# Pack attention with a soft mixture of experts on one core: the third duo's sums, the token shares and the PSUM banks are put in other places

## The chip, the cores and the metric

The kernel runs on one core of a Trainium2 chip. The metric is the device time of one execution in microseconds (us). The five engines of the core have these names in the profile: PE (TensorE, matmuls), DVE (VectorE), ACT (ScalarE), POOL (GpSimd) and SP (SyncE), which issues all the transfers here. In the trace each engine runs its instructions in the order in which the program lists them, so an instruction that waits holds up what is listed behind it on that engine.

## The reference

```python
def attn(q, k, v, p):                 # q, k, v: 8 x 8 x 576 x 64, p: 8 x 8 x 32 x 64
    s = p @ k^T / 8;   a = softmax(s);   pp = a @ v         # pack: 32 rows per head
    s = q @ pp^T / 8;  a = softmax(s);   return a @ pp      # unpack: 576 rows per head
x = attn(...) as 4608 tokens x 512
logits = x @ phi                      # 4608 x 32 slots
d = softmax of logits over the tokens (axis 0)
slot_in = d^T @ x                     # 32 x 512; 4 slots belong to each of 8 experts
slot_out[e] = max(slot_in[e] @ w1[e], 0) @ w2[e]            # w1: 512x1024, w2: 1024x512
c = softmax of logits over the slots (axis 1)
out = c @ slot_out                    # 4608 x 512, float32
```

The tokens x are never formed: the logits are taken as a @ (pp @ phi), and the slot inputs are summed as d^T @ a, times pp.

## The kernel before

**Steps and duos.** The batch of 8 is worked through in four duos of two batches (`dd` = 0 to 3), and each duo in two steps of four heads (8 steps, `i` = 0 to 7, `ND` = 4). A step loads k, v and q, makes pack scores (L229), their softmax, the packed rows (L297), transposes q (L386), makes unpack scores (L430), their softmax (L457 to L480: maximum, difference, exponential on ACT, row sum and reciprocal on DVE, product on POOL), transposes the shares (L491, L502) and makes logits (L518, added up into `LT` by L535).

**Duo sums.** After the second step of a duo the softmax over the tokens goes on as a running one. F1, F2, F2d: maximum `mt` of the duo's logits, a transpose `mx` of it on PE, and a new running maximum `m4` with the difference `dm`. F3, F3d, F3x: two tiny matmuls `my` spread them over the partitions, DVE negates them (`nmg`), and ACT takes the exponentials `dL` with row sums `zg`. F4d: DVE transposes `dL` into `dz` and forms `rw`. F4: matmul `mz` adds up the row sums. F5: the logits are transposed into `L_sb`. GR: 36 matmuls `gr` (L654) multiply `dz` with the duo's shares. RTa, RTd: `gr` is copied to `rt` by ACT and by DVE. GT, GB, GS, GSA: two more small matmuls with a product `rb` between them, whose result is added to `S_run`. GZ keeps `z_run`, the running divisor; in the last duo it also scales `hm` and `S_run` by its reciprocal. After the last duo L921 puts `S_run` plus the last `gs` into `xz`, the experts' inputs; this is the last step before the experts.

**The order** of all these steps is written out by hand in the text `ORDER`, one word per step, and everything that a step issues goes on its engines in that order. The first step of duo 0's sums stands behind step 3's logits, of duo 1's behind step 5's. The loads of the weights are issued as slots of a ring of 14 tiles, or memory of tiles no longer needed (`GIVE`), come free.

**Token shares.** `c1`, `c2`, `c3` make the softmax of `L_sb` over the slots (two reductions of 1152 elements per partition, L937 and L949, a difference, an exponential, a product), `cq` splits it in two parts, and `cp` transposes it, four transposes (L1062) into one PSUM bank and a copy into `cT`; there are nine such groups.

**Experts.** `layer1a` (matmuls `hp`, L982) and `layer2` (`so`, L1031) go through 8 experts; `hidden` and `layer1b` copy and transpose between them. Expert 7's second layer is made in two halves (`sb`, L1108), then `sr` (L1121, L1129) adds up partitions, and `sh` is the slot output. The code from `layer1a` to `sh` keeps the order in which it is written.

**Output.** 36 tiles of 128 tokens: a matmul `op` of 128x512 (L1145; the first tile in two halves, L1162), a copy from PSUM by ACT or DVE (L87, L90, in the helper `evac`, which gives each copy to the engine with the smaller sum of estimated costs), and transfers of 1 MB from `ob`, the last two of 0.5 MB from `ot`. This part is not ordered by hand: a scheduler places its instructions, and did so with the last seven groups of `cp`.

**PSUM** has eight banks of 128x512. Before the experts: one pair of banks `m` (pool `psm`) and three rotating pairs (pool `prs`). In the experts and the output: two rotating pairs in pool `psa` (for `hp`, `sb`, `sr`, `op`), one bank for `so`, three single banks in pool `pstr` (for `ht`, `cp`). A pair is handed on only as a whole.

Of the kernel before, what the change touches and what calls it, by code (L numbers as in the profile page):

```python
# [20 lines left out]
def pack_attention_soft_moe(  # L21
# [586 lines left out]
    def f4(dd):  # L608
        x = du[dd]
        x["zp"] = pair(prs, f"mz_{dd}")[:, 0, 0:NSLOT]  # L610
        nc.tensor.matmul(x["zp"], ones, x["rw"], start=True, stop=True)
# [127 lines left out]
    def load_w(pool, lay, e, c):  # L739
# [92 lines left out]
        XQA.2 PREP.2 N2.1 MP.2 MXb.3 MM.2 S1a.3 EXb.3 MXa.3 QC.2 A2P.1 XQC.2 EXa.3 KT1.4 A2T.1
        S2.2 KT0.4 QE.3 AP.3 MT.2 MS.2 AT.3 A1T.3 LG.1 A1U.3 QC.3 PPM.3 XQC.3 E2.2 LT.1 F1.0
        F2.0 PPN.3 QA.3 F2d.0 QB.3 XQA.3 Z.2 F3.0 S1a.4 XQB.3 S1b.4 F3d.0 MXa.4 N2.2 F3x.0 F4d.0
        EXa.4 PT.3 MXb.4 PPT.3 F4.0 GR.0 QE.4 KT0.5 EXb.4 PRP.3 MP.3 RTa.0 AP.4 MM.3 PREP.3
        RTd.0 GZ.0 A1T.4 GT.0 KT1.5 S2.3 GB.0 GS.0 MT.3 AT.4 GSA.0 A2P.2 F5.0 A1U.4 MS.3 PPM.4
        A2T.2 QC.4 LG.2 E2.3 PPN.4 QB.4 LT.2 QE.5 Z.3 PT.4 XQC.4 XQB.4 QA.4 XQA.4 S1a.5 N2.3
        PPT.4 S1b.5 MXa.5 MP.4 EXa.5 MXb.5 MM.4 A2P.3 EXb.5 KT1.6 S2.4 A2T.3 KT0.6 AP.5 MT.4
        MS.4 AT.5 A1T.5 LG.3 A1U.5 QC.5 PPM.5 QE.6 XQC.5 E2.4 LT.3 F1.1 F2.1 PPN.5 QA.5 F2d.1
        QB.5 XQA.5 Z.4 F3.1 S1a.6 XQB.5 S1b.6 F3d.1 MXa.6 N2.4 F3x.1 F4d.1 EXa.6 PT.5 MXb.6  # L840
        PPT.5 F4.1 GR.1 KT0.7 EXb.6 MP.5 RTa.1 AP.6 MM.5 RTd.1 GZ.1 GT.1 A1T.6 S2.5 KT1.7 GB.1
        GS.1 MT.5 AT.6 GSA.1 A2P.4 F5.1 A1U.6 MS.5 PPM.6 A2T.4 QC.6 LG.4 E2.5 PPN.6 QE.7 QA.6
        LT.4 Z.5 PT.6 XQC.6 QB.6 PPT.6 XQA.6 MP.6 S1a.7 MM.6 XQB.6 N2.5 S1b.7 MXa.7 S2.6 EXa.7
        MXb.7 EXb.7 QA.7 MT.6 MS.6 AT.7 AP.7 A1U.7 XQA.7 QC.7 A1T.7 E2.6 A2P.5 PPM.7 XQC.7 Z.6
        A2T.5 QB.7 N2.6 PPN.7 LG.5 XQB.7 LT.5 PT.7 PPT.7 F1.2 F2.2 MP.7 F2d.2 MM.7 A2P.6 S2.7
        A2T.6 MS0.7 F3.2 LG.6 LT.6 MT.7 E20.7 MS1.7 E21.7 F3d.2 Z0.7 F3x.2 N20.7 Z1.7 A2P0.7
        N21.7 A2T0.7 A2P1.7 F4d.2 F5.2 A2T1.7 F4.2 GZ.2 LG.7 LT.7 GR.2 F1.3 F2.3 RTd.2 RTa.2
        GT.2 F2d.3 F3.3 GB.2 GS.2 F3d.3 F3x.3 GSA.2 F4d.3 F4.3 F5.3 GZ.3 GR.3 RTa.3 RTd.3 GT.3
        GB.3 GS.3 GSA.3
# [55 lines left out]
    with tc.manual_schedule(engines={EP.PE, EP.DVE, EP.Activation, EP.Pool}):  # L905
# [15 lines left out]
        nc.vector.tensor_tensor(  # L921
# [53 lines left out]
    def layer1a(e0, es):  # L975
        if e0 == es[0]:
            hp = pair(psa, f"hp_{e0}")
            hss[e0] = [hp[:, 0], hp[:, 1]]
        hp = hss[e0]
        for e in es:  # L980
            for nh, a in ((nh, 2 * c + y) for c in range(2) for nh in range(2) for y in range(2)):
                nc.tensor.matmul(  # L982
                    hp[nh][32 * a : 32 * a + 32, :],
                    xzf[:, (4 * e + a) * NSLOT : (4 * e + a + 1) * NSLOT],
                    w1s[e, a // 2][:, a % 2, nh * 512 : (nh + 1) * 512],
                    start=(e == e0),
                    stop=(e == e0 + QE - 1),
                )
# [222 lines left out]
```

## Time and profile before

| | |
|---|---|
| Time, median of 3 runs | 240.16 us (239.95 to 242.99) |
| The profiled execution | 241.48 us, span from first to last instruction 239.7 us |
| Busy | PE 192.1 us (80%), DVE 137.5 (57%), ACT 89.7 (37%), POOL 31.2 (13%) |
| Moved | 72.84 MB, of which 9.44 MB is output; mean 304 GB/s |
| Mean granted PE clock | 0.876 |

How to read it: the profiled execution's time is its span plus 1.8 us around it, and every duration below is from that one execution. The granted clock is the share of its full speed that PE was given; eight transposes of 128x128 took 1.09 us at a clock of 1.00 (at 134.8 us), four took 1.11 us at 0.50 (at 143.9 us). Start times are counted from the start of the span.

### The profile page before, as it was taken

What the parts mean: (1) busy time and instruction counts of PE and PEld (TensorE: products, weight loads), DVE (VectorE), ACT (ScalarE), POOL (GpSimd) and SP (SyncE); (2) the same over time, 40 slices, a digit from 0 to 9 for tenths busy, and PEclk for the clock granted to TensorE, in tenths of its full rate; (3) what the DMA queues carried; (4) which work ended last, traced back from release to release, by engine and by line L of the source; (5) the groups of instructions that cost most, each with busy time, mean ns of one, the idle gap of its engine ahead of it and who ended that gap; (6) DMA issues with size and microseconds to landing.
All of it is one profiled execution on the core that took longest, in us unless ns stands there. A gap on an engine that the chain in (4) does not pass through costs nothing.

```text
span 239.7 us, 6484 instructions
## 1 busy us (share of the span) xinstructions
PE 192.1 (80%) x2795; PEld 128.6 (54%) x2795; DVE 137.5 (57%) x280; ACT 89.7 (37%) x174; POOL 31.2 (13%) x42
## 2 busy tenths in 40 slices
PE   0569977899879999979998627874999999688960
PEld 0247666777649777769786515772233344233320
DVE  2563786678596689767776486396312634433240
ACT  2041736374472473643667332102020010444520
POOL 6103000521060030020223010100030000000000
PEclk9999999999997999979999995757899999855555
DMA  5999999999999999995592990086499992278767
GB/s 155 385 338 349 390 391 270 390 389 326 345 389 391 391 406 407 407 374 187 198 355 72 424 383 5 0 299 228 130 421 428 418 415 118 72 282 347 298 278 304
DMA packets 27037, 72.84 MB, mean 304 GB/s; under 512 B 6400, under 2 KB 6656, under 8 KB 24192
## 3 DMA queue, kind: packets, MB, share of 16 engines
q1 hardware_dynamic: 27008, 72.42, 81.7%
q8 instruction: 22, 0.36, 0.6%
q14 instruction: 7, 0.06, 0.1%
HBM read 62.98 MB, written 9.44 MB: 302 GB/s over the span
## 4 chain that ended last, share of the span: by engine, by line
PE 52%; DMA 18%; DVE 14%; ACT 8%; issue 3%; SPq 1%; POOL 0%; DVEq 0%; ACTq 0%
DMA pn<-in_p_dram 8%; PE gr L654 7%; PE hp L982 7%; DMA k<-in_k_dram 6%; PE op L1145 6%; PE so L1031 5%; PE m L297 5%; PE s L430 4%; PE s L229 4%; DMA q<-in_q_dram 4%; PE a2p L491 3%; PE ap L263 2%; DVE ob L90 2%; ACT ob L87 2%; DVE kT L212 2%
## 5 line engine op out<-in xcount | busy, mean ns | idle before, releaser
L229 PE MATMUL s<-kT,pT 32*32 32x288 f32 x512 | 20.7, 458 | 9.2 <-DVE kT L212 8.7
L1145 PE MATMUL op<-sh,cT 128*128 128x512 f32 x35 | 23.1, 744 | 2.9 <-DVE ob L90 1.3
L480 POOL TENSOR_TENSOR a<-a,z 128x1152 f32<-128x1152 f32 (+1 forms) x8 | 15.9, 1992 | 61.7 <-DVE nmg L588 19.0
L212 DVE STREAM_TRANSPOSE kT<-k 128x1152 f32<-128x1152 f32 x16 | 21.4, 1358 | 0.2
L297 PE MATMUL m<-v,a1T 64*64 64x128 f32 x576 | 19.8, 291 | 0.7 <-ACT a1T L287 0.4
L250 ACT ACTIVATE a<-s,nm 128x576 f32<-128x576 f32 x16 | 11.9, 742 | 19.5 <-DVE nm L240 13.4
L297 PEld LDWEIGHTS m<-v,a1T 64*64 64x64 f32 x576 | 17.5, 144 | 3.1 <-issue 1.2
L240 DVE TENSOR_REDUCE nm<-s 128x1 f32<-128x576 f32 x16 | 12.0, 755 | 11.1 <-PE s L229 11.1
L1145 PEld LDWEIGHTS op<-sh,cT 128*128 128x128 f32 x35 | 9.8, 279 | 15.8 <-ACT ob L87 7.3
L386 PE MATMUL qp<-ident,q 128*128 128x128 f32 x128 | 16.7, 276 | 1.2 <-issue 1.2
L229 PEld LDWEIGHTS s<-kT,pT 32*32 32x32 f32 x512 | 9.0, 111 | 15.6 <-DVE kT L212 9.6
L90 DVE COPY ob<-op 128x512 f32<-128x512 f32 (+1 forms) x13 | 8.6, 670 | 14.0 <-PE op L1145 13.5
L87 ACT COPY ob<-op 128x512 f32<-128x512 f32 (+1 forms) x20 | 11.4, 575 | 13.5 <-PE op L1145 11.7
L654 PE MATMUL gr<-a,dz 128*64 128x128 f32 x144 | 16.4, 398 | 0.0
L982 PE MATMUL hp<-w,xz 128*32 128x512 f32 x128 | 16.0, 649 | 0.5 <-DVE xz L921 0.5
L430 PE MATMUL s<-ppT,qT 128*64 128x64 f32 x512 | 16.3, 222 | 0.1
L391 ACT COPY qT<-qp 128x1024 f32<-128x1024 f32 x16 | 15.9, 1021 | 0.7 <-PE qp L386 0.6
L386 PEld LDWEIGHTS qp<-ident,q 128*128 128x128 f32 x128 | 14.0, 141 | 3.3 <-issue 2.7
L654 PEld LDWEIGHTS gr<-a,dz 128*64 128x64 f32 x144 | 15.2, 206 | 1.1 <-issue 0.9
L430 PEld LDWEIGHTS s<-ppT,qT 128*64 128x64 f32 x512 | 15.6, 138 | 0.2 <-ACT a L250 0.2
L491 PE MATMUL a2p<-ident,a 128*128 128x128 f32 x64 | 9.7, 296 | 5.5 <-POOL a L480 4.5
L457 DVE TENSOR_REDUCE mx<-s 128x32 f32<-128x1024 f32 (+1 forms) x9 | 9.9, 1096 | 6.0 <-PE s L430 6.0
(144 smaller groups left out, 283.0 us busy)
## 6 DMA issues: line engine op xcount, KB each, us to landing
w<-in_moe_w_dram SPq DMA_DIRECT2D x31, 1024.0 KB, 10.7
k<-in_k_dram SPq DMA_DIRECT2D x16, 576.0 KB, 8.4
v<-in_v_dram SPq DMA_DIRECT2D x16, 576.0 KB, 10.3
q<-in_q_dram SPq DMA_DIRECT2D x16, 576.0 KB, 11.6
out_dram<-ob SPq DMA_DIRECT2D x7, 1024.0 KB, 3.9
pn<-in_p_dram SPq DMA_DIRECT2D x16, 64.0 KB, 8.0
w<-in_moe_w_dram SPq DMA_DIRECT2D x2, 512.0 KB, 16.9
out_dram<-ot SPq DMA_DIRECT2D x2, 512.0 KB, 5.3
```

What stands on the lines that cost most here:

```text
L87: nc.scalar.copy(dst, src)
L212: nc.vector.transpose(st[i]["kT"][:, b2].rearrange("p a t x r -> p (a t x r)"), kts[i][:, b2].rearrange("p a x -> p (a x)"),)
L229: nc.tensor.matmul(ps[32 * c : 32 * c + 32, u, 0:HALF], pTs[dd][rs, b2, g, a, x], kT[rs, b2, a, :, x, :], start=(x == 0), stop=(x == 1),)
L297: nc.tensor.matmul(s["m"][64 * b2 : 64 * b2 + 64, y, 0:P], s["a1T"][rs, t, 64 * b2 : 64 * b2 + 64], vt[rs, b2, :, t * D : (t + 1) * D], st ...
L386: nc.tensor.transpose(tp[:, o : o + P], qts[i][:, b2, a, j * P : (j + 1) * P], ident)
L391: nc.scalar.copy(flat(qT(i)[:, 8 * b2 : 8 * b2 + 8]), st[i][f"qp{b2}"])
L430: nc.tensor.matmul(pv[64 * b2 : 64 * b2 + 64, j, h], s["qT"][:, 8 * b2 + 4 * a + j, R * y : R * y + R], ppT[:, b2, h], start=True, stop=True,)
L480: eng.tensor_tensor(a2, a2, st[i][f"z{t0}"].unsqueeze(3).broadcast_to([P, n, 4, NS]), op=ALU.mult)
L491: nc.tensor.transpose(s["ap2"][:, t * P : (t + 1) * P] if t < 8 else s["lp"][:, 1, 0:P], s["a2"][:, t].rearrange("p h s -> p (h s)"), ident,)
L654: nc.tensor.matmul(x["gb"][64 * c : 64 * c + 64, g * P : (g + 1) * P], dz[:, t].rearrange("p b s -> p (b s)"), a2[:, t].rearrange("p h s - ...
L982: nc.tensor.matmul(hp[nh][32 * a : 32 * a + 32, :], xzf[:, (4 * e + a) * NSLOT : (4 * e + a + 1) * NSLOT], w1s[e, a // 2][:, a % 2, nh * 5 ...
L1145: nc.tensor.matmul(op, cT[:, o, :], sh, start=True, stop=True)
```

## The change

**Order of the duo sums.** In duos 0 and 1, F3 to F4d stand earlier, right behind F2d and between the two halves of q's transposes, and GR stands ahead of F4. In duo 2, F3 to F4d stand ahead of the last step's softmax, and GR, F4, GT, GB and GS are placed among the steps of that softmax, where they stood behind it. In duo 3 likewise F4d is followed by F5 and GR, and only then come F4 and GZ. `mz` of duo 2 now takes the pair `m` (`psm`). On PE, from the first duo (`qp` are transposes of q, `s_4` pack scores, `ap` transposes of shares):

```order
-L386 MATMUL qp_1_983<-ident,q_185 128x128 x8
-L575 MATMUL my_999<-ones,m_0_979 128x1
-L229 MATMUL s_4_0_1001<-kT_840,pT_788 32x288 x16
-L229 MATMUL s_4_1_1019<-kT_840,pT_788 32x288 x16
+L575 MATMUL my_983<-ones,m_0_979 128x1
+L386 MATMUL qp_1_988<-ident,q_185 128x128 x8
+L229 MATMUL s_4_0_1010<-kT_840,pT_788 32x288 x16
+L229 MATMUL s_4_1_1028<-kT_840,pT_788 32x288 x16
 L341 MATMUL m_903<-ident,ppd_966 128x128 x2
-L611 MATMUL mz_1057<-rw_1046,ones 128x32
-L654 MATMUL gr_1059<-a_0_434,dz 64x128 x9
-L654 MATMUL gr_1059<-a_1_620,dz 64x128 x9
```

`my` has moved ahead of the second eight transposes of q, and behind these rows `gr` comes first and `mz` after it. Around the last softmax PE had, before (`s_7` are the last unpack scores, `a2p_2132` the transposes of the last shares, `lp_2133` the last logits, `gr_2163` duo 2's sums, `mx_2188` the transposed maximum of duo 3):

```order
-L430 MATMUL s_7_2050<-ppT,qT_1915 64x2x32 x32
-L575 MATMUL my_2099<-ones,m_2_2030 128x1
-L583 MATMUL my_2099<-dm_2032,ones 128x32
-L518 MATMUL lp_2039<-a2T_2093,mm_1814 32x288 x4
-L491 MATMUL a2p_2132<-ident,a_7_2049 128x128 x8
-L491 MATMUL lp_2133<-ident,a_7_2049 128x128
-L611 MATMUL mz_2153<-rw_2148,ones 128x32
-L518 MATMUL lp_2133<-a2T_2139,mm_2036 32x288 x4
-L654 MATMUL gr_2163<-a_4_1350,dz 64x128 x9
-L654 MATMUL gr_2163<-a_5_1628,dz 64x128 x9
-L548 MATMUL mx_2188<-ident,mt_2186 1x128
```

And now, for the same stretch (the two rows of `my` of duo 2 stand ahead of `s_7`, not shown):

```order
+L430 MATMUL s_7_2064<-ppT,qT_1915 64x2x32 x32
+L658 MATMUL gr_2116<-a_4_1350,dz 64x128 x9
+L658 MATMUL gr_2116<-a_5_1628,dz 64x128 x9
+L518 MATMUL lp_2053<-a2T_2110,mm_1814 32x288 x4
+L615 MATMUL mz_2149<-rw_2050,ones 128x32
+L681 MATMUL gr_2116<-repb,rt_2117 64x32 x8
+L491 MATMUL a2p_2172<-ident,a_7_2063 128x128 x8
+L491 MATMUL lp_2173<-ident,a_7_2063 128x128
+L714 MATMUL gr_2116<-rb_2118,ppd_1243 64x64 x2
+L714 MATMUL gr_2116<-rb_2118,ppd_1472 64x64 x2
+L518 MATMUL lp_2173<-a2T_2178,mm_2046 32x288 x4
+L548 MATMUL mx_2205<-ident,mt_2203 1x128
```

The big `gr` of duo 2 stood between the last logits and duo 3's `mx`; it now stands right behind the last scores.

**Token shares** are tied behind L921: the first reduction of `c1` may not be placed ahead of it on DVE. It stood, with the three instructions that follow it, among the steps of duo 3's GZ and GB; now L923 (`xz`) stands ahead of all of them.

**PSUM in the experts and the output.** The two pairs and three single banks become seven single banks in one pool. With that the scheduler places the seven groups of `cp` in another part of the program. On PE there were 28 transposes between the second layer's last weights; the rows from there to `sh` now read:

```order
+L1037 MATMUL so<-w_6_0_2314,hT 32x512 x4
+L1037 MATMUL so<-w_6_1_2316,hT 32x512 x4
+L1112 MATMUL sb_2528<-w_7_0_2318,hT 32x256 x4
+L1112 MATMUL sb_2529<-w_7_0_2318,hT 32x256 x4
```

and the seven groups stand among the output's matmuls, in twos or singly behind every fourth or fifth `op`, with their copies among the output's copies on ACT and DVE.

```diff
     def f4(dd):
         x = du[dd]
-        x["zp"] = pair(prs, f"mz_{dd}")[:, 0, 0:NSLOT]
+        if dd == ND - 2:
+            mz = psm.tile([P, 2, 512], F32, tag="m", name=f"mz_{dd}")
+        else:
+            mz = pair(prs, f"mz_{dd}")
+        x["zp"] = mz[:, 0, 0:NSLOT]
...
-        A2T.6 MS0.7 F3.2 LG.6 LT.6 MT.7 E20.7 MS1.7 E21.7 F3d.2 Z0.7 F3x.2 N20.7 Z1.7 A2P0.7
+        F4d.2 A2P.6 S2.7 MT.7 A2T.6 MS0.7 GR.2 E20.7 LG.6 MS1.7 RTa.2 E21.7 F4.2 LT.6 Z0.7 N20.7
...
-        nc.vector.tensor_tensor(
+        xz_add = nc.vector.tensor_tensor(
             xz[:, :, 0 : 4 * NSLOT].rearrange("p e (h s) -> p e h s", h=4)[:, :, :, 0:SPE],
...
-        psa = ctx.enter_context(tc.tile_pool(name="psa", bufs=2, space=psum))
         pso = ctx.enter_context(tc.tile_pool(name="pso", bufs=1, space=psum))
-        pstr = ctx.enter_context(tc.tile_pool(name="pstr", bufs=3, space=psum))
+        pstr = ctx.enter_context(tc.tile_pool(name="pstr", bufs=7, space=psum))
...
-        nc.vector.tensor_reduce(cm[:, a:b], Lf[:, a:b], axis=AX.X, op=ALU.max)
+        top = nc.vector.tensor_reduce(cm[:, a:b], Lf[:, a:b], axis=AX.X, op=ALU.max)
+        tc.add_manual_dep(top.ins, xz_add.ins.name, ...)
...
-            hp = pair(psa, f"hp_{e0}")
-            hss[e0] = [hp[:, 0], hp[:, 1]]
+            hss[e0] = [bank(pstr, f"hp_{e0}_{nh}") for nh in range(2)]
...
-    def slot_out(dst, n, o, x):
-        if x == 0:
-            ops[0] = pair(psa, f"op_{n}")
-        op = ops[0][:, x]
+    def slot_out(dst, n, o):
+        op = bank(pstr, f"op_{n}")
         nc.tensor.matmul(op, cT[:, o, :], sh, start=True, stop=True)
         evac(dst, op)
```

`sb`, `sr` and the first tile's two halves take single banks in the same way.

More of the change, by code (lines that the diff above doesn't have):

```diff
@@ L832, in pack_attention_soft_moe @@
[L832 to L843, printed above, removed]
@@ L844, in pack_attention_soft_moe @@
[L844 to L849 removed]
+        A1T.0 S1a.1 PPM.0 MXa.1 EXa.1 PPN.0 S1b.1 QE.0 MXb.1 PT.0 QB.0 PPT.0 EXb.1 KT0.2 MP.0 QA.0
@@ new lines, in pack_attention_soft_moe @@
+        F1.1 F2.1 PPN.5 QA.5 F2d.1 F3.1 XQA.5 F3d.1 QB.5 F3x.1 Z.4 F4d.1 S1a.6 XQB.5 S1b.6 MXa.6
+        N2.4 EXa.6 PT.5 MXb.6 PPT.5 GR.1 F4.1 KT0.7 EXb.6 MP.5 RTa.1 AP.6 MM.5 RTd.1 GZ.1 GT.1 A1T.6
+        S2.5 KT1.7 GB.1 GS.1 MT.5 AT.6 GSA.1 A2P.4 F5.1 A1U.6 MS.5 PPM.6 A2T.4 QC.6 LG.4 E2.5 PPN.6
+        QE.7 QA.6 LT.4 Z.5 PT.6 XQC.6 QB.6 PPT.6 XQA.6 MP.6 S1a.7 MM.6 XQB.6 N2.5 S1b.7 MXa.7 S2.6
+        EXa.7 MXb.7 EXb.7 QA.7 MT.6 MS.6 AT.7 AP.7 A1U.7 XQA.7 QC.7 A1T.7 E2.6 A2P.5 PPM.7 XQC.7 Z.6
@@ L850, in pack_attention_soft_moe @@
+        A2T.5 QB.7 N2.6 PPN.7 LG.5 XQB.7 LT.5 F1.2 PT.7 F2.2 F2d.2 PPT.7 F3.2 F3d.2 MP.7 F3x.2 MM.7
+        F4d.2 A2P.6 S2.7 MT.7 A2T.6 MS0.7 GR.2 E20.7 LG.6 MS1.7 RTa.2 E21.7 F4.2 LT.6 Z0.7 N20.7
+        RTd.2 Z1.7 GT.2 N21.7 A2P0.7 A2T0.7 A2P1.7 GB.2 A2T1.7 GS.2 GZ.2 GSA.2 F5.2 LG.7 LT.7 F1.3
+        F2.3 F2d.3 F3.3 F3d.3 F3x.3 F4d.3 F5.3 GR.3 F4.3 GZ.3 RTa.3 RTd.3 GT.3 GB.3 GS.3 GSA.3
     """
@@ L936, in c1 @@
     def c1(a, b, eng=nc.vector):
-        nc.vector.tensor_reduce(cm[:, a:b], Lf[:, a:b], axis=AX.X, op=ALU.max)
+        top = nc.vector.tensor_reduce(cm[:, a:b], Lf[:, a:b], axis=AX.X, op=ALU.max)
+        tc.add_manual_dep(
+            top.ins,
+            xz_add.ins.name,
+            mybir.DependencyInfo(mybir.DependencyClass.NoSync, mybir.DependencyReason.SCHED_ONLY),
+            reason="the experts' inputs go first",
+        )
         eng.tensor_tensor(
@@ L1095, in pack_attention_soft_moe @@
         halves = [slice(x * DM // 2, (x + 1) * DM // 2) for x in range(2)]
-        sb2 = pair(psa, "sb")
-        sb = [sb2[:, x] for x in range(2)]
+        sb = [bank(pstr, f"sb{x}") for x in range(2)]
         so2 = extras[0].tile([P, 2, DM], F32, tag="ring", name="sot")
@@ L1102, in pack_attention_soft_moe @@
         shf = sh.bitcast(F32)
-        sr2 = pair(psa, "sr")
-        srs = [sr2[:, 0], sr2[:, 1]]
+        srs = [bank(pstr, f"sr{x}") for x in range(2)]
         repf = rep.rearrange("p c s -> p (c s)")
@@ L1157, in pack_attention_soft_moe @@
                 if (dd, o) == (0, 0):
-                    op0 = pair(psa, "op_0")
-                    for x, (xs, eng) in enumerate(zip(halves, ("act", "dve"))):
-                        op = op0[:, x]
+                    for xs, eng in zip(halves, ("act", "dve")):
+                        op = bank(pstr, f"op_0_{eng}")
                         nc.tensor.matmul(op[:, xs], cT[:, k_, :], sh[:, xs], start=True, stop=True)
@@ L1174, in pack_attention_soft_moe @@
                     cp(todo.pop(0), None)
-        slot_out(ot[:, dd], f"{dd}", dd * T + T - 1, (dd == 0))
+        slot_out(ot[:, dd], f"{dd}", dd * T + T - 1)
     for y in range(2):
```

19 lines of the change are left out of this document (12 added, 7 removed).

## The prediction

> **What bounds the kernel now.** First the page's DMA share in 40 slices of 6 us, and the busy time by stage; then the chain of work that ended last. Of the stage rows I use the PE busy time (the first number behind the length) and the last three columns: granted clock, DMA share, GB/s.
>
> ```profile
> DMA  5999999999999999995592990086499992278767
> ```
>
> ```profile
> 140.00:142.00 2.00, 0.00 (x0) 0.00 (x0) 1.97 (x5) 0.84 (x2) 0.00 (x0) 1.00 0.98 389
> 190.00:192.00 2.00, 2.00 (x24) 0.71 (x20) 0.22 (x1) 0.00 (x0) 0.00 (x0) 1.00 1.02 418
> 220.00:222.00 2.00, 1.74 (x3) 0.86 (x3) 0.72 (x2) 0.98 (x2) 0.00 (x0) 0.50 0.96 393
> 236.00:238.00 2.00, 0.00 (x0) 0.00 (x0) 0.00 (x0) 0.00 (x0) 0.00 (x0) 0.50 1.03 385
> ```
>
> ```profile
> 147.75 1.19 PE lp L518 x8
> 148.94 4.33 PE gr L654 x36
> ...
> 163.97 1.35 DVE cm L949
> ...
> 199.40 0.86 PE sb L1108 x16
> 200.27 1.08 PE sr L1121 x4
> 201.35 1.06 PE sb L1108 x14
> ...
> 205.92 0.37 PE op L1162
> ...
> 211.02 0.81 PE op L1145
> 211.85 0.60 ACT ot L87
> 212.49 0.81 PE op L1145
> ```
>
> No single engine bounds the whole. Up to about 107 us the transfers are full, though from 70 us the chain runs through PE. From 139 to 167 us it is a string of small steps, with PE idle in the last softmax and transfers at zero from 144 to 156 us. From 171 to 199 us PE and the weights' stream (418 GB/s) run side by side. From 206 us PE works at half clock and waits, tile by tile, for copies; then 2 MB of output drain. The change touches all but the stream.
>
> **A. Duos 0 and 1.** PE rows of the timeline (start, length; in brackets the idle time before and who ended it), and PE's clock in half-microseconds (busy time and count, clock, DMA share, GB/s):
>
> ```profile
> 66.18 0.35 PE L575 MATMUL my<-ones,m 1*128 1x1 f32 x2 [0.40 <-DVE m L560]
> 70.49 0.41 PE L611 MATMUL mz<-rw,ones 128*128 128x32 f32 x2 [1.36 <-DVE rw L606]
> 70.83 4.07 PE L654 MATMUL gr<-a,dz 128*64 128x128 f32 x36
> 99.11 0.35 PE L575 MATMUL my<-ones,m 1*128 1x1 f32 x2 [0.16 <-DVE m L563]
> 103.72 0.38 PE L611 MATMUL mz<-rw,ones 128*128 128x32 f32 x2 [1.72 <-DVE rw L606]
> 104.03 3.47 PE L654 MATMUL gr<-a,dz 128*64 128x128 f32 x36
> ```
>
> ```profile
> 71.00:71.50 0.50, 0.50 (x8) 0.54 1.17 415
> ...
> 74.50:75.00 0.50, 0.50 (x20) 1.00 1.05 392
> 104.50:105.00 0.50, 0.50 (x14) 1.00 1.04 418
> 105.00:105.50 0.50, 0.50 (x12) 0.68 1.02 401
> ```
>
> The chain `my`, `nmg`, `dL`, `dz` now starts eight transposes earlier, so `dz` is ready when PE gets to `gr`, and the idle 1.36 and 1.72 us go. But `my` itself now reaches PE about 0.95 us before its input, since only half the transposes stand ahead: its waits grow from 0.40 to 1.35 and from 0.16 to 1.1. Net 0.4 + 0.8 = 1.2 us. `mz` only changes sides. Clock: the gaps were followed by half clock from 71.0 and 105.2 us, under which `gr` runs about 8 matmuls per half-microsecond against 14. At full clock the two `gr` would take some 2.5 us each (estimate between 4.07 x 8 / 14 = 2.3 and what missing records leave open) and save 2.6 us together. The new gaps at `my` are nearly as long as the old ones, so I count a third: **A = 2.0**. Bounds: 0 (the gaps merely change places, the exponentials of the next pack softmax hold its transposes) and 3.8.
>
> **B. From the last scores to the experts.**
>
> ```profile
> 134.19 0.27 PE L548 MATMUL mx<-ident,mt 128*1 128x128 f32 x1 [0.50 <-DVE mt L541]
> 134.81 0.28 DVE L563 TENSOR_TENSOR m<-mr,m_run 1x128 f32<-1x128 f32 x1
> ...
> 143.94 1.11 PE L491 MATMUL a2p<-ident,a 128*128 128x128 f32 x4 [4.53 <-POOL a L480]
> ...
> 149.57 0.45 DVE L541 TENSOR_REDUCE mt<-LT 128x1 f32<-128x288 f32 x1
> ...
> 153.18 0.27 PE L548 MATMUL mx<-ident,mt 128*1 128x128 f32 x1
> ...
> 157.46 0.60 PE L611 MATMUL mz<-rw,ones 128*128 128x32 f32 x2 [1.76 <-DVE rw L606]
> ...
> 157.99 4.53 PE L654 MATMUL gr<-a,dz 128*64 128x128 f32 x36
> ...
> 160.39 0.17 DVE L627 TENSOR_SCALAR z_run<-z_run 128x32 f32<-128x32 f32 x1
> ...
> 161.35 0.29 DVE L636 TENSOR_TENSOR S_run<-S_run,al 128x128 f32<-128x128 f32 x1
> ...
> 165.24 0.48 DVE L688 TENSOR_TENSOR rb<-gr,hm 128x128 f32<-128x128 f32 x2
> ...
> 166.69 3.57 PE L982 MATMUL hp<-w,xz 128*32 128x512 f32 x16 [0.46 <-DVE xz L921]
> ```
>
> Costs first. `my` of duo 2 now stops PE from 134.46 until `m` (135.1) is there and takes some 0.6 (two halves, 0.35 for the first in A): the last scores end 1.25 us later. In the softmax PE has `gr`, `lp` of step 6, `mz` and `gt` ahead of the shares' transposes; at full clock these fit in the 4.53 us in which PE waited for POOL. On POOL the clearing of `xz`, released by `gr`, now stands ahead of the product N20; the half of `gr` that releases it should end some 2 us before N20's input is there, which covers it. The `rt` copies on ACT and DVE add a little. In return the softmax loses the DVE steps F3d, F4d and F5 that stood in it, and PE, busy, should keep its clock: the transposes (1.11 for four at half clock) halve. I let these cancel: the last logits end at 148.9 as now. Bounds: 0.6 earlier, 2.0 later.
>
> Gains: `mx` no longer waits for `gr`: mt ends at 150.02, `mx` started at 153.18: 3.15. Copies and `rb` (0.48) leave DVE between `mx` and `nmg`: 0.55. `gr` starts behind `dz`, without `rw` and `mz` ahead: 0.85. So `gr` starts 4.55 us earlier. Behind it a new wait takes the place of the old one. The old: L949 (163.97, 1.35 us) ran ahead of `rb`, which came 1.25 later for it. The new: `mz` (0.60) behind `gr`, and DVE's chain from z_run to `S_run` (160.39 to 161.64, with the add ahead of it 1.45) ahead of the `rt` copy, which so starts 2.05 behind `gr`'s end where it started about 0.4 behind it: 1.65. Net loss 0.4. **B = 4.55 - 0.4 = 4.1**; bounds 2.0 and 5.5 (a full clock in `gr` would add more). The experts thus start 6.1 us earlier, and the stream with them, since its slots come free as `hp` consumes.
>
> **C. The end of the experts.**
>
> ```profile
> 194.37 2.31 PE L1062 MATMUL cp<-identr,c 128*128 128x128 f32 x21
> ...
> 198.95 0.84 PEld L1108 LDWEIGHTS sb<-w,hT 128*32 128x32 f32 x16 [0.46 <-DMA w<-in_moe_w_dram]
> ```
>
> 28 transposes, 3.1 us of PE, leave this place; but `sb` waited for weights at 198.95 even so: the stream sets this end, and its waits hid the transposes. 0.3 is won. Without them PE waits there for weights, 1.0 to 1.5 us at a time (a 1 MB piece takes 2.5 us at 418 GB/s, its eight matmuls 0.9, half of 3.57 / 2, as L982's rows ran at half clock). Gaps of that size were followed by half clock twice in A. If so, `sb`, `sr`, `sb` (0.86, 1.08, 1.06) take up to twice as long: -3.0. I take **C = -0.8**.
>
> [...]
>
> **D. The output.**
>
> ```profile
> 211.55 0.29 PEld L1145 LDWEIGHTS op<-sh,cT 128*128 128x128 f32 x1 [0.25 <-DVE ob L90]
> ...
> 232.62 1.43 SPq L1178 DMA_DIRECT2D out_dram<-ot  x2
> ```
>
> Now a pair of tiles takes 1.47 us (211.02 to 212.49), as the pair's bank is free only when both are copied; inside a pair the second follows after 0.53. With seven banks PE need not wait: 35 x 0.53 = 18.6 us at half clock. Added: 28 transposes, 0.11 us each in C, 0.22 at half clock: 6.2 us, and seven copies, which ACT and DVE (0.60 and about 0.7 a copy, a third busy) hide. So PE needs 24.7 instead of 26.2 us even at half clock. But then it is dense, and dense stretches (`gr` at 71 to 74.5) brought the clock back after some 3.4 us. From then on the output transfers bound: the second megabyte can go out at about 6.7 us (eight tiles, eight transposes, a copy), the other 8.4 MB need 21 us at 400 GB/s (between 385 and 418), and the drain shows about 1.9 us on top (2.1 MB from 232.6 to 239.7). That is 29.6 us behind 205.9, against 33.8: **D = 4.2**. Bounds: 1.5 (half clock throughout) and 5.4.
>
> **Sum.** 2.0 + 4.1 - 0.8 + 4.2 = 9.5 us. The profiled execution took 241.48 (span 239.7); it becomes 232.0. The median of the runs is 1.3 lower, so the forecast is 240.16 - 9.5 = **230.7**, chance 0.50.
>
> **Rivals.**
> 1. The clock stays low to the end: A and B as above, C -3.0, D 1.5: 240.16 - 4.6 = **235.6**, chance 0.18. For it: the clock was 0.50 through the whole output; against: PE never was dense there. [...]
> 2. The softmax is held up: `gr` of duo 2 at half clock (4.4 us) pushes the last shares' transposes, logits 3 us later, B = 1.0: **233.8**, chance 0.12.
> 3. The full clock holds in the `gr` of duos 0 to 2 and the stream of output runs at 418: A 3.5, B 5.0, C 0.3, D 5.4: **226.0**, chance 0.14.
> 4. Slower: PE stays at half clock wherever work was moved, and a tile's pace is set by matmul plus copy, 0.735 us, not by banks. Then the 6.2 us of transposes come on top of the output (D = -6.2), C -3.0, A 1.2, B 2.0: **246.2**, chance 0.06. It decides once a tile's pace stays above 0.735 - 6.2 / 35 = 0.56 us.
>
> The change could also simply not take hold in D: the order shows the transposes between the `op`, so that is excluded; no chance goes to it.
>
> **Range and chances.** 226.0 to 236.5 leaves out rival 4 and parts of 1 and 3, under 2 in 10. About 2% (4.8 us, 235.4) is what a measurement of this kernel can tell from no change: faster holds the forecast, rivals 2 and 3 and a little of 1, 0.79; same most of 1 and the small results between, 0.16; slower 0.05.
>
> **What would show it.** A: `gr` of duos 0 and 1 without idle time ahead, `my` with more than a microsecond, clock near 1.00. B: `mx` of duo 3 within 0.5 us of `mt`; `hp` starting near 160.6; POOL's product not waiting for the clearing. C: idle time "<-DMA w" ahead of the last `so` and `sb`; the clock there. D: the clock back at 1.00 within 7 us, DMA share near 1.0 from then on, the drain unchanged. Wrong would be a later end of the last logits (B), or an output whose tiles still come every 0.7 us.

## The result, and the profile after

The changed kernel took 232.5 us (median of four runs, 230.97 to 236.4) beside 240.69 us of the kernel before in the same session; the ratio of the two is 0.962, 95% interval 0.951 to 0.974. (The ratios here are taken over the executions within 1.5% of the fastest of their kernel, the medians over all.) In a second session it took 233.36 us, ratio 0.966 (0.962 to 0.970). The profiled execution took 233.84 us with a span of 232.0 us, 7.7 us less than the span of before. The forecast was 230.7 us.

First the total's place in time. The chain of work that ended last, as in the prediction (start, length, what it was):

```profile
166.75 9.94 PE hp L988 x80
...
198.41 1.07 PE sb L1112 x16
...
200.54 1.03 PE sb L1112 x16
...
204.13 0.39 PE op_dve L1161
...
```

`hp` starts at 166.75; before it was 166.69. So up to the experts nothing was won. The first tile's second half starts at 204.13 instead of 205.92, and behind it lie 27.9 us to the end of the span instead of 33.8. Stages, in us, from the starts of the named rows on PE's timeline (before, after, gain):

| stretch | before | after | gain | forecast |
|---|---|---|---|---|
| A: `mx` to next `ap`, duo 0 | 63.77 to 75.08 | 64.74 to 75.06 | +1.0 | |
| A: the same, duo 1 | 96.94 to 107.80 | 96.46 to 108.50 | -1.2 | +2.0 for both |
| B: `mx` of duo 2 to `hp` | 134.19 to 166.69 | 134.53 to 166.75 | +0.3 | +4.1 |
| C: `hp` to the first tile's second half | 39.2 | 37.4 | +1.9 | -0.8 |
| D: from there to the end | 33.8 | 27.9 | +5.9 | +4.2 |
| the rest, which was not edited | | | -0.2 | 0 |

The sum is 7.7 against 9.5: near enough in total, but from other parts than the forecast said. A and B, where it saw 6.1 us, brought nothing in this execution; C and D, where it saw 3.4, brought 7.7. A depends on the execution: in the profile of the second session both `gr` ran at full clock (2.40 us each), and the two stretches of A took 20.6 us instead of the 22.2 of before.

**The output** in stages of 2 us, columns as in the prediction (busy PE, PEld, DVE, ACT, POOL, granted clock, DMA share, GB/s):

```profile
206.00:208.00 2.00, 2.00 (x15) 1.72 (x14) 1.98 (x4) 2.00 (x5) 0.00 (x0) 1.00 0.16 51
208.00:210.00 2.00, 2.00 (x15) 1.60 (x13) 2.00 (x5) 2.00 (x6) 0.00 (x0) 1.00 1.01 384
220.00:222.00 2.00, 0.00 (x0) 0.00 (x0) 0.00 (x0) 0.00 (x0) 0.00 (x0) 0.56 0.97 397
```

In the first two rows PE, DVE and ACT are busy nearly throughout and the clock is 1.00, and from 208 us the transfers are full to 229 us (mean share 1.01). At 220 us PE has long been done, where before it was in the middle of its work at a clock of 0.50. The output is now bound by the transfers.

**The last softmax**, PE rows of the timeline of the changed kernel (in brackets the idle time before a row and who ended it):

```profile
133.58 0.44 PE L341 MATMUL m<-ident,ppd 128*128 128x128 f32 x2 [1.78 <-DVE ppd L326]
134.53 0.27 PE L548 MATMUL mx<-ident,mt 128*1 128x128 f32 x1 [0.50 <-DVE mt L541]
135.57 0.55 PE L575 MATMUL my<-ones,m 1*128 1x1 f32 x2 [0.78 <-DVE m L563]
136.90 1.97 PE L491 MATMUL a2p<-ident,a 128*128 128x128 f32 x8
139.49 3.06 PE L430 MATMUL s<-ppT,qT 128*64 128x64 f32 x64
142.38 2.35 PE L658 MATMUL gr<-a,dz 128*64 128x128 f32 x36
...
151.15 1.19 PE L518 MATMUL lp<-a2T,mm 128*32 128x288 f32 x8
153.57 0.37 PE L548 MATMUL mx<-ident,mt 128*1 128x128 f32 x1 [1.23 <-DVE mt L541]
...
157.74 4.50 PE L658 MATMUL gr<-a,dz 128*64 128x128 f32 x36 [1.99 <-DVE dz L604]
```

and the same scores before, where they ended at 138.23:

```profile
134.78 1.09 PE L491 MATMUL a2p<-ident,a 128*128 128x128 f32 x8
136.19 2.04 PE L430 MATMUL s<-ppT,qT 128*64 128x64 f32 x64
```

From 134.93 us the granted clock is 0.50, and it comes back at 141.75: the eight transposes take 1.97 instead of 1.09 us, the scores 3.06 instead of 2.04, and they end at 142.55, 4.3 us later than before (4.0 counted from `mx`). The forecast had 1.25. The clock fell ahead of `my`'s new wait of 0.78 us, behind two holes of 1.78 and 0.50 us that before had too, of the same size (at 133.25 and 134.19). There it did not fall (1.00 from 134 to 140 us); what decides it is not shown. What the new order adds is that `my`, its wait, the transposes and all the scores now lie behind these holes.

### The profile page after: what moved, and what is told of

Same layout as the page of the kernel before. It is cut to its first block, busy times and chain, and to the rows that moved or that the text cites. A ratio compares the mean times of both kernels' runs of the same rounds, so it can differ in the third digit from the quotient of the medians.

```text
span 232.0 us, 6492 instructions
## 1 busy us (share of the span) xinstructions
PE 179.4 (77%) x2795; PEld 126.0 (54%) x2795; DVE 138.8 (60%) x280; ACT 88.3 (38%) x174; POOL 31.2 (13%) x42
## 5 line engine op out<-in xcount | busy, mean ns | idle before, releaser
L229 PE MATMUL s<-kT,pT 32*32 32x288 f32 x512 | 21.5, 482 | 8.8 <-DVE kT L212 8.4
L430 PE MATMUL s<-ppT,qT 128*64 128x64 f32 x512 | 18.9, 240 | 0.0
L430 PEld LDWEIGHTS s<-ppT,qT 128*64 128x64 f32 x512 | 18.1, 156 | 0.2 <-ACT a L250 0.2
L386 PE MATMUL qp<-ident,q 128*128 128x128 f32 x128 | 17.1, 277 | 1.2 <-issue 1.2
L229 PEld LDWEIGHTS s<-kT,pT 32*32 32x32 f32 x512 | 9.5, 113 | 15.1 <-DVE kT L212 9.4
L658 PE MATMUL gr<-a,dz 128*64 128x128 f32 x144 | 13.6, 348 | 2.0 <-DVE dz L604 2.0
L658 PEld LDWEIGHTS gr<-a,dz 128*64 128x64 f32 x144 | 12.5, 179 | 2.6 <-issue 2.6
L1037 PE MATMUL so<-w,hT 128*32 128x512 f32 x112 | 12.6, 593 | 1.0 <-DMA w<-in_moe_w_dram 1.0
L473 DVE TENSOR_REDUCE z<-a 128x36 f32<-128x1152 f32 (+2 forms) x9 | 10.9, 1209 | 1.9 <-ACT a L467 1.9
L467 ACT ACTIVATE a<-a 128x1152 f32<-128x1152 f32 (+2 forms) x9 | 9.6, 1061 | 6.1 <-DVE a L458 5.2
L279 ACT COPY a1T<-ap 128x1024 f32<-128x1024 f32 x8 | 8.1, 1018 | 8.1 <-PE ap L263 8.1
## 6 DMA issues: line engine op xcount, KB each, us to landing
q<-in_q_dram SPq DMA_DIRECT2D x16, 576.0 KB, 12.4
```

The lines of the kernel that those rows point to most:

```text
L229: nc.tensor.matmul(ps[32 * c : 32 * c + 32, u, 0:HALF], pTs[dd][rs, b2, g, a, x], kT[rs, b2, a, :, x, :], start=(x == 0), stop=(x == 1),)
L386: nc.tensor.transpose(tp[:, o : o + P], qts[i][:, b2, a, j * P : (j + 1) * P], ident)
L430: nc.tensor.matmul(pv[64 * b2 : 64 * b2 + 64, j, h], s["qT"][:, 8 * b2 + 4 * a + j, R * y : R * y + R], ppT[:, b2, h], start=True, stop=True,)
L658: nc.tensor.matmul(x["gb"][64 * c : 64 * c + 64, g * P : (g + 1) * P], dz[:, t].rearrange("p b s -> p (b s)"), a2[:, t].rearrange("p h s - ...
L1037: nc.tensor.matmul(so[32 * a : 32 * a + 32, :], hTf[:, (NJ * e + j) * NSLOT : (NJ * e + j + 1) * NSLOT], w2s[e, j // 4][:, j % 4, :], star ...
```

## The experiments

Two theories were put to the test, besides the forecast's own: that the single banks bring nearly all, and that the new order's gain in the last softmax is eaten by the fallen clock.

**1. The banks alone, and the order alone.** `banks_only` is the kernel before with `psa` removed and `pstr` at seven banks; nothing of `ORDER`, `f4` or the tie. `order_only` is the rest of the change, with the old pairs.

```diff
-        psa = ctx.enter_context(tc.tile_pool(name="psa", bufs=2, space=psum))
-        pstr = ctx.enter_context(tc.tile_pool(name="pstr", bufs=3, space=psum))
+        pstr = ctx.enter_context(tc.tile_pool(name="pstr", bufs=7, space=psum))
```

> The kernel before with nothing but the single PSUM banks (which also move the seven cp groups). Theory 1, the forecast's terms: the order is worth some 6 us and the banks 3.4, so 240.5 - 3.4 = 237. Theory 2, read off the two traces (experts start at 166.7 in both, first output matmul 1.8 us earlier, output 33.8 -> 27.9 us): the banks are worth nearly all, 7.7 us, so 233, with hp starting near 166.7, the first op near 204 and 28 us from there to the end.

> The changed order and the tie, with the old pairs of PSUM banks. Theory 1: 240.5 - 6.1 = 234.5, hp starting near 160.6. Theory 2: between 239 and 241, as the half clock around the last scores eats the order's gain; hp starting near 166.7, the output 33 to 34 us long. [...]

Measured: the banks alone 231.88 us, ratio 0.963 (0.959 to 0.966); the order alone 239.6 us, ratio 0.994 (0.990 to 0.997). Of the theories on record, Theory 2 has both times within about 1 us; with the banks alone the output took 27.4 us from the first op, and `hp` came at 164.63, 2 us ahead of its mark. The times of the order alone lie mostly near 239 and near 242 us, with mean clocks of 0.88 and 0.86. In the profile of the order alone (an execution of 242.32 us; PE rows), `op` still comes in pairs:

```profile
205.79 0.39 PE L1170 MATMUL op<-sh,cT 128*128 128x256 f32 x1 [0.92 <-DVE sh L1140]
206.75 0.35 PE L1170 MATMUL op<-sh,cT 128*128 128x256 f32 x1 [0.57 <-DVE sh L1140]
206.94 0.39 PE L1153 MATMUL op<-sh,cT 128*128 128x512 f32 x1
207.62 0.97 PE L1153 MATMUL op<-sh,cT 128*128 128x512 f32 x2 [0.29 <-DVE ob L90]
```

Each pair waits 0.2 to 0.3 us for a copy, and from the first op to the end lie 34.7 us, as before. So alone the banks bring 9.0 us, and the order 1.3 (0.6 to 2.4 by its interval), which is under the 2% that count as a difference here; beside the banks, in the same session, nothing (233.36 us with it, 231.88 without).

**2. The changed kernel again, and with the transposes put back** between the last experts' matmuls.

```diff
-        layer2(2, E - 1)
+        layer2(2, E - 2)
+        for t0 in range(8, 28, 4):
+            cp(t0, None)
+        layer2(E - 2, E - 1)
+        for t0 in (28, 32):
+            cp(t0, None)
...
-    todo = list(range(8, NT, 4))
+    todo = []
```

> The changed kernel once more, for the spread of its times and clocks. Theory 2: 231 to 234 throughout, hp starting at 166 to 167. Theory 3: two groups, near 231 (clock 0.92) and near 234 (clock 0.90); if this profile is of the first group, hp starts near 163.5 to 164 and the last scores end near 139.5 at full clock.

> The changed kernel with the seven cp groups back between the second layer's last matmuls, banks single. If the stream of weights sets the experts' end and the output's transfers set the output's length: the same time within 1 us, first op within 0.4 us of the changed kernel's relative to hp, output 27 to 28.5 us. If taking the transposes out of the experts had won the 1.8 us there: 1.5 to 2 us slower at the first op. If the transposes cost the output: 1 to 2 us shorter there.

Measured: 233.36 us (231.2 to 235.01), and 231.1 us with the transposes back (230.47 to 231.85), ratio 0.959 (0.956 to 0.962). The repeated run's profile (231.2 us) is of Theory 3's lower group, but its marks are not: `hp` came at 164.63, the scores were at half clock (mean 0.52 from 135 to 140 us), and from `mx` of duo 2 to `hp` it was 32.4 us as in the first profile. What it had won was A. The transposes' new place among the output is no gain; put back they cost nothing in the experts (first op 37.2 us behind the first `hp`, 37.5 with them in the output) and the output is 0.7 us shorter, 26.6 us from the first op. The medians differ by 2.3 us, more than these stretches explain.

**3. What in the banks.** `banks4` keeps the number of banks of before: four single banks for `hp`, `sb`, `sr`, `op`, three for the transposes.

```diff
-        psa = ctx.enter_context(tc.tile_pool(name="psa", bufs=2, space=psum))
+        psa = ctx.enter_context(tc.tile_pool(name="psa", bufs=4, space=psum))
...
-            ops[0] = pair(psa, f"op_{n}")
-        op = ops[0][:, x]
+        op = bank(psa, f"op_{n}")
```

> The kernel before with single banks for hp, sb, sr and op, as in banks_only, but from a pool of four banks of their own (as many as the two pairs of before had), with the transposes' three beside it instead of one pool of seven. Theory 1 (what cost the time was that two engines' copies share one tile of two banks, so that a matmul waits for both): output from the first op to the end 27 to 28.5 us, clock 1.00 in it, time 231 to 233. Theory 2 (it is the depth of seven that lets PE run ahead): PE waits for copies again, clock at half at the start of the output, 31 to 35 us from the first op, time 236 to 240.

Measured: 233.07 us, ratio 0.967 (0.963 to 0.972), with 26.7 us from the first op to the end. Timeline of PE, and a stage of it:

```profile
204.49 0.38 PE L1152 MATMUL op_act<-sh,cT 128*128 128x256 f32 x1 [0.49 <-DVE sh L1127]
...
205.14 9.23 PE L1136 MATMUL op<-sh,cT 128*128 128x512 f32 x27
```

```profile
208.00:210.00 2.00, 1.91 (x7) 1.09 (x7) 1.29 (x2) 1.99 (x4) 0.00 (x0) 1.00 1.09 430
```

27 matmuls without an idle row between them, at full clock, and the transposes are among the experts here as they were before. It was not the depth of seven but the tile of two banks: as long as one copy of a pair was open, the other bank could not be had. How much of the longer output was this wait and how much the half clock that came with it, no run parts. The same shows outside PE. Copies of `sb`, `sr` on DVE and ACT, before and then after:

```profile
202.43 0.42 DVE L1126 COPY sot<-sb 128x256 f32<-128x256 f32 x1 [2.27 <-PE sb L1108]
202.89 0.37 ACT L1127 COPY sos<-sb 128x256 f32<-128x256 f32 x1 [6.54 <-DVE sot L1126]
204.94 0.37 ACT L1131 CAST sh<-sr 128x256 fp32r<-128x256 f32 x1 [0.49 <-DVE sh L1132]
```

```profile
201.59 0.42 DVE L1130 COPY sot<-sb 128x256 f32<-128x256 f32 x1 [3.95 <-PE sb L1112]
201.65 0.37 ACT L1131 COPY sos<-sb 128x256 f32<-128x256 f32 x1 [17.70 <-PE sb L1112]
202.81 0.81 ACT L1135 CAST sh<-sr 128x256 fp32r<-128x256 f32 x2 [0.78 <-PE sr L1133]
```

Before, ACT's copy of its half of `sb` waited for DVE's copy of the other half, and its second cast waited for DVE's work on the first. With a tile for each bank the two run side by side. From the end of the second `sb` to the first tile's second half it is 3.57 us in both kernels with pairs, and 2.57 or 2.58 in all twelve profiles with single banks.

**4. Duos 0 and 1 set back** to the old order in the changed kernel.

```diff
-        ... F2d.0 F3.0 XQA.3 F3d.0 QB.3 F3x.0 Z.2 F4d.0 S1a.4 ... GR.0 F4.0
+        ... F2d.0 QB.3 XQA.3 Z.2 F3.0 S1a.4 XQB.3 S1b.4 F3d.0 ... F4.0 GR.0
```

> The changed kernel with the order of before in duos 0 and 1 alone; the last two duos, the tie and the single banks stay. Theory 1 (my ahead of the scores costs 0.7 us a duo at an equal clock, the forecast's +2.0 us was a matter of the clock in that one execution): mx to the next ap of duo 0 9.6 us with gr at full clock or 11.3 at half, against 10.3 and 12.0 in the changed kernel; time 0.5 to 1.5 us less than the changed kernel, 230.5 to 232. Theory 2 (the forecast's term, duos 0 and 1 gain 2 us by the order): 11 us or more with gr at half clock in both duos, time 2 us above the changed kernel, 233.5 to 235.

Measured: 231.99 us, ratio 0.959 (0.954 to 0.964), not to be told from the changed kernel. The rows of duo 0, in the changed kernel:

```profile
67.17 0.35 PE L575 MATMUL my<-ones,m 1*128 1x1 f32 x2 [1.28 <-DVE m L560]
...
70.72 2.40 PE L658 MATMUL gr<-a,dz 128*64 128x128 f32 x36
73.55 0.41 PE L615 MATMUL mz<-rw,ones 128*128 128x32 f32 x2 [0.43 <-ACT a L250]
```

and with the old order in this run, where `gr` was at half clock:

```profile
66.13 0.35 PE L575 MATMUL my<-ones,m 1*128 1x1 f32 x2 [0.40 <-DVE m L560]
70.77 4.06 PE L658 MATMUL gr<-a,dz 128*64 128x128 f32 x36
```

Over all profiles of this study, the stretch from `mx` to `ap` has four lengths only, but for 10.86 us in duo 1 of before: old order 9.65 to 9.68 us with `gr` at 2.40 and 11.29 to 11.36 with `gr` near 4.0; new order 10.30 to 10.32 and 12.0. At an equal clock the new order is 0.7 us longer, since `my`, `mz` and what follows wait: in duo 0 of the changed kernel, PE's idle time in the stretch is 2.5 us (1.28 and 0.43 ahead of these two, 0.23 and 0.53 ahead of the next, `m` and `ap`), where it was 1.8 (0.40 and 1.36). It has the full clock more often, in 13 of 16 such stretches against 5 of 12. Means over these few executions: 10.64 against 10.59 us. Theory 1, 0.7 us a duo lost at an equal clock, holds; the forecast's gain from the clock is there too, in part of the executions; over these few they cancel.

**5. Holding the clock in the last softmax.** In the changed kernel PE was given work that nothing reads, transposes of a constant into the second bank of `mx` and `my` of duo 2: 12 ahead of PT of the last pair, 5 ahead of F3.

```diff
+    def fill(tile, n):
+        for j in range(n):
+            o = (j % 4) * P
+            nc.tensor.transpose(tile[:, 1, o : o + P], ident, ident)
...
-        ... LT.5 F1.2 PT.7 F2.2 F2d.2 PPT.7 F3.2 ...
+        ... LT.5 F1.2 WA.2 PT.7 F2.2 F2d.2 PPT.7 WB.2 F3.2 ...
```

> The changed kernel with 17 more TensorE transposes of a 128 by 128 constant: 12 ahead of the last duo's PT, 5 ahead of duo 2's second row sums (F3.2), written into halves of PSUM tiles that nothing reads. They fill the holes of 0.8 to 1 us after mx and before my of duo 2. Theory 1 (the clock falling to half at 134.96 us is what ate the gain of the new order in the last softmax): granted clock 1.00 in 133 to 139, the last pair's second scores end 2.5 to 4 us earlier than in the changed kernel, from mx of duo 2 to the first hp 29 to 30.5 us instead of 32.2 to 32.5, time 229 to 231 (changed kernel 231 to 233.5). Theory 2 (the clock is a side effect; the chains between DVE, ACT and PE behind the scores set the start of the experts): scores earlier, but mx to hp within 0.7 us of 32.3, time within 1 us of the changed kernel, or up to 1.5 us more by the fillers' own 17 times 0.06 to 0.12 us. If the fillers don't hold the clock, it falls at 133 to 137 as before and neither theory is tried.

Measured: 229.91 us, ratio 0.955 (0.951 to 0.959). PE rows:

```profile
132.02 0.27 PE L576 MATMUL mx<-ident,mt 128*1 128x128 f32 x1 [0.41 <-DVE mt L541]
132.13 0.71 PE L547 MATMUL my<-ident 128*128 128x128 f32 x5
...
133.79 1.09 PE L491 MATMUL a2p<-ident,a 128*128 128x128 f32 x8
135.20 2.04 PE L430 MATMUL s<-ppT,qT 128*64 128x64 f32 x64
...
161.37 8.85 PE L1023 MATMUL hp<-w,xz 128*32 128x512 f32 x56 [0.45 <-DVE xz L958]
```

From `mx` to the end of the scores it is 5.2 us instead of 8.0, and from `mx` to `hp` 29.35 instead of 32.2: Theory 1. The same marks over the profiles of the study, in us behind `mx` of duo 2:

| kernels | clock at the scores | scores end | last logits end | last logits to `hp` | `hp` |
|---|---|---|---|---|---|
| old order: before | full | 4.0 | 14.75 | 17.75 | 32.5 |
| old order: `banks_only`, `banks4`, `old_best` | half at first (in `old_best` from 133.52 to 136.93) | 5.5 to 5.6 | 16.3 | 15.7 to 18.1 | 32.0 to 34.4 |
| new order: the changed kernel (twice), `order_only`, `cps_back` | half | 8.0 to 8.3 | 17.8 to 18.1 | 14.4 | 32.2 to 32.5 |
| new order: `after_no01`, `after_untie` | half, back within the scores | 6.8 to 6.9 | 17.1 | 13.8 to 14.3 | 30.8 to 31.4 |
| new order with the 17 fillers: `warm_softmax`, `warm_cps` | full | 5.2 | 15.0 to 15.2 | 14.1 to 14.4 | 29.4 |

So the old order loses by the fall of the clock too, where it comes (1.5 us), the new one more (2.8), and behind the logits the new order is ahead in every row. In this run another place took some of it back, the one of the forecast's term C: the first op came 39.6 us behind `hp`, not 37.5 as in the repeated run of the changed kernel, as the clock fell at 193.97 (the 40.24 us of the expectation below is to the third row of `op`). PE's row there, at nearly twice its length:

```profile
194.16 1.93 PE L1147 MATMUL sb<-w,hT 128*32 128x256 f32 x16 [1.54 <-DMA w<-in_moe_w_dram]
```

**6. The fillers with the transposes back,** `warm_cps` (experiments 5 and 2 together), **and fillers in the whole last softmax,** `warm_all_cps`: 40 more, ahead of F2, F3 and GR of duo 3 and behind its GZ, GT and GS.

> The kernel with the 17 filling transposes ahead of PT of the last duo and of duo 2's second row sums, and beside it the seven groups cp put back between the last experts' matmuls. In the run with the fillers alone the experts began 29.35 us after mx of duo 2 instead of 32.2, but PE then waited .62 and 1.54 us for weights at 191 and 193, the clock fell to .50 from 194 to 197.4 and the first op came 40.24 us after the first hp instead of 37.5. Theory 1 (the fallen clock at the end of the experts costs these 2.7 us): cp's transposes fill the two waits, clock 1.00 in 190 to 200, first op 37.2 to 38 us after hp, time 227 to 229. Theory 2 (the stream of weights sets the end whatever PE does): first op within 0.7 us of the same distance from the last weights' landing, time as with the fillers alone, 229.5 to 231.

> As warm_cps, with 40 more filling transposes ahead of F2, F3 and GR of duo 3 and behind GZ, GT and GS, so that PE has work in the holes of 1.2, 0.8, 2.0 and 1.8 us of 145 to 160. Theory 1 (half clock, not the chains, sets the rest of the last softmax too): gr of duo 3 2.4 us instead of 4.2 to 4.5, mx of duo 2 to hp 26.5 to 28 us, time 225 to 227.5. Theory 2 (behind the last scores DVE, ACT and POOL are the bound): gr shorter, but the first hp no more than 2 us earlier by it; the weights' stream then starts earlier by as much and the time is 227 to 229. If the fillers themselves delay the matmuls queued behind them, hp comes later than in warm_cps.

Measured: 228.79 us (226.72 to 230.64), ratio 0.948 (0.935 to 0.961), and 223.87 us (223.18 to 227.47), ratio 0.935 (0.928 to 0.942). In the first, `cp` fills PE's wait for weights, and `sb` runs at full clock; the first op is 37.0 us behind `hp` instead of 39.6, which is Theory 1. The whole time shows less: three of the six executions took 226.7 to 227.2 us and three 230.4 to 230.6, and the interval of the ratio covers that of the fillers alone.

```profile
192.12 0.88 PE L1103 MATMUL cp<-identr,c 128*128 128x128 f32 x8
193.02 1.07 PE L1152 MATMUL sb<-w,hT 128*32 128x256 f32 x16
```

In the second, `mx` of duo 2 to `hp` is 27.4 us, and the `gr` of duo 3 runs at full clock, which is Theory 1 again:

```profile
135.61 0.27 PE L576 MATMUL mx<-ident,mt 128*1 128x128 f32 x1 [0.41 <-DVE mt L541]
...
156.29 2.40 PE L687 MATMUL gr<-a,dz 128*64 128x128 f32 x36 [0.66 <-DVE dz L632]
...
163.04 7.53 PE L1023 MATMUL hp<-w,xz 128*32 128x512 f32 x68
```

Its profiled execution took 227.47 us, with the `gr` of duo 0 at half clock. By its median this is the fastest version of the study: 57 matmuls that compute nothing take 7.2 us off the kernel with the transposes back (231.1), measured in another session, which puts into a number what half clock had cost in the last softmax.

**7. The tie alone taken away** from the changed kernel.

```diff
-        top = nc.vector.tensor_reduce(cm[:, a:b], Lf[:, a:b], axis=AX.X, op=ALU.max)
-        tc.add_manual_dep(top.ins, xz_add.ins.name, ...)
+        nc.vector.tensor_reduce(cm[:, a:b], Lf[:, a:b], axis=AX.X, op=ALU.max)
```

> The changed kernel without the tie: the token shares' maxima, subtraction, sums and reciprocal stand ahead of the experts' inputs on DVE again. Theory 1 (the forecast's: they hold DVE for 1.2 us an operation just where gr of duo 3 ends, so the inputs come late): the first hp 1 to 3 us later after mx of duo 2 than 32.3 us, time 233 to 236. Theory 2 (they fit into the 5 to 6 us in which DVE waits for gr_3, so the tie is worth nothing while PE is at half clock): hp within 0.5 us of the changed kernel, time 231 to 233.5.

Measured: 233.12 us, ratio 0.971 (0.962 to 0.980), `mx` to `hp` 31.4 us: no later than with the tie, but the scores got their clock back sooner here (64 matmuls in 2.47 us instead of 3.06); from the last logits it is 14.3 us against 14.4. Theory 2: the token shares fit into DVE's waits for `gr`, all but L950, behind which `rb` starts 1.46 us after the copy of `rt` instead of 1.04. Those 0.4 us can't be seen in the time. Whether the tie is worth more where the clock is held was not run.

**8. Two candidates on the old order.** `old_best` has the single banks, the transposes back and the second output MB in pieces (`n = 1 if dd == 0 else TB`); `old_warm` the single banks, the transposes back and 76 fillers in the old order's holes.

> A candidate: order of before throughout, no tie, single banks from the pool of seven, the seven groups of transposes back between the last experts' matmuls, and the second output MB sent in pieces of 256 KB too. If Theory 2 of the first runs holds (the banks bring all, the order nothing or a loss), 229.5 to 231; if the order brings something beside the banks, 231.5 to 233. If the start of the output is limited by the wait for whole MBs, the DMA share between first op and 10 us later is nearer 1 than in banks_only and the output takes 25.5 to 26.5 us from the first op; if by the bytes, 26.6 to 27.4 as before.

> The order of before, single banks, cp between the last experts' matmuls, and 76 filling transposes in that order's holes (12 ahead of PT, 5 ahead of F3 of duo 2, 30 ahead of the last pair's a2p where PE waits 4.5 us for POOL, 10 ahead of mz of duo 3, 6, 10 and 3 around rt and rb). It asks whether the forecast's step for the last softmax (the new order lets the experts start earlier) holds where the clock is held in both orders. Theory 1 (it does; only the clock had eaten it): mx of duo 2 to the first hp 29.5 to 32 us against 27.4 in the new order with all fillers, time 225.5 to 229 against 223.9. Theory 2 (the clock is all, the order nothing): 26.5 to 28 us, time 222.5 to 224.5.

Measured: 231.48 us, ratio 0.963 (0.958 to 0.968), and 229.88 us (226.42 to 232.12), ratio 0.947 (0.939 to 0.954). The first lies between its two ranges and decides nothing. Its smaller pieces changed nothing: the output took 27.0 us from the first op, with a DMA share of 0.83 in the first 10 us as in `banks_only`. The second was to part order and clock; it met neither theory's ranges, with `hp` 32.4 us behind `mx`:

```profile
133.06 0.27 PE L577 MATMUL mx<-ident,mt 128*1 128x128 f32 x1 [0.41 <-DVE mt L541]
...
141.93 6.39 PE L547 MATMUL my<-ident 128*128 128x128 f32 x30 [2.86 <-ACT al L626]
148.15 0.60 PE L491 MATMUL a2p<-ident,a 128*128 128x128 f32 x4
...
165.47 4.95 PE L1015 MATMUL hp<-w,xz 128*32 128x512 f32 x44
```

The 30 fillers waited 2.86 us for ACT to read the other bank of `my`'s pair, took 0.21 us each (6.39 in all) where the ten at 156.38 took 0.13, so at half clock for part of them, and held the shares' transposes up: the last logits end 18.6 us behind `mx`, worse than in any other run. Behind them `hp` comes after 13.8 us, with the clock held (`gr` of duo 3 in 2.40 us). In `warm_all_cps` they take 12.4 us, so behind the logits the new order gains 1.4 us. Ahead of them it loses 1.2 at the end of the scores (5.2 us behind `mx` against 4.0 in before). With the 14.75 us that the logits took in before, 13.8 makes 28.6 us for the old order, an estimate, beside 27.4. It is an upper end: in before the clock was full at the scores, but half from 142.72 on, through the transposes of the shares and the last logits. So with the clock held the order is worth about a microsecond or less; no run shows it, and it stays open.

## Why the prediction was right, and where it was not

The total was right within 1.8 us, and its sign; of its four parts only D came as worked, and larger. That the total came out so near is luck: A and B fell 6.0 us short, and C and D brought 4.3 more than forecast.

**A was mis-sized: -0.2 here, 0 by the means of experiment 4, where it had +2.0.** What was to be seen was seen: `gr` has no idle time ahead, and its clock is 1.00 in duo 0. `my`'s wait came with 1.28 and 1.03 us as forecast. What failed is the net of 1.2 us: `mz`, which "only changes sides", and `ap` got waits for ACT's exponentials (0.43 and 0.53 us in duo 0), the lower bound's reason, and at an equal clock the net is a loss of 0.7 a duo. The clock's gain is 1.7 us a duo by experiment 4, but it comes in only some executions, with either order.

**B failed in its first cost, the scores' end 1.25 us later.** That sum took the transposes and scores at their old length, at full clock; the clock fell ahead of them, and they ended 4.3 us later. "PE, busy, should keep its clock", said of the softmax behind, came true for part of it: the clock was full from 141.75 to 148.58, and `gr` of duo 2 and the first four of the shares' transposes ran at it. So the last logits came at 152.34 instead of 148.94, where the forecast let gains and losses cancel; this is the sign of being wrong that it had named itself. The rest of B stood: `mx` of duo 3 came 1.23 us behind the last logits where it had been 4.24, a gain of 3.0 against the 3.15 forecast; the wait behind `gr` grew by 0.3 against 0.4. Between them, `mx` to `gr`, 0.6 was won instead of 1.4, with `my` at half clock. -3.4, +3.0, +0.6 and -0.3 make next to nothing. With the clock held (experiment 5) the steps came out as worked: scores 1.2 us later than before (forecast 1.25), logits 0.3 to 0.5 (forecast 0), `hp` 3.1 us earlier behind `mx` (forecast 4.1). Rival 2 had the right loss, logits 3 us later, by another way: it had `gr` of duo 2 at half clock, which ran at 2.35 us.

**C: the fear did not come true here, and a gain was missed.** The waits for weights were there, 0.97 and 1.53 us, and the clock stayed at 1.00 through them; in experiment 5 it fell at the same place, at 193.97. That the stream sets this end and hides the transposes was right. What the forecast had not seen is that ACT and DVE stopped waiting for each other at `sb` and `sr` (experiment 3): 2.6 us instead of 3.6 to the first tile. The other 0.9 us of C lie ahead of the first `sb`, 31.7 us behind `hp` instead of 32.5; the repeated run has 32.2, so this part is not shown to be the change's.

**D was right in its mechanism and too small.** The clock was at 1.00 from the first op, as at `sb`, and not only within 7 us, so transfers were full 4 us behind the first tile instead of 6.7. The bound behind it, 8.4 MB at some 400 GB/s, is what the stage rows show, and 27.9 us against 29.6. Rival 4's tile pace was off by more than two: 27 tiles in 9.23 us in `banks4` are 0.34 us each. Rival 1's low clock did not come: with shared pairs the clock fell once in the output, at 207.58 in before, and stayed at 0.50 to the end; with single banks, whether four or seven, it stayed at 1.00 as long as PE worked in the output.

## What to carry to other kernels

Give every PSUM bank that two engines read a tile of its own (the single banks alone took 9.0 us off here), and look in the trace for copies that wait for a copy and not for a matmul. When work is moved, ask of each new wait on PE not only how long it is but what it does to the clock of what follows: here two holes of 2.3 us together cost up to 2.8 us more behind them, in the executions in which the clock fell. Where a short string of dependent steps can't be shortened, harmless matmuls in its holes can be the cheapest change in the kernel: 17 of them brought `hp` from 32.2 to 29.35 us behind `mx` here.
